# A pre-LN FNet and GEGLU block on one core: an eighth pass of the sequence DFT as seven block products, its operand sums moved to GpSimd

## The chip, the cores and the metric

The kernel runs on one core of one Trainium2 chip. The metric is the device time of one execution in microseconds (us), the median of several runs. In the profile PE is TensorE (its matmuls), PEld its weight loads, DVE is VectorE, ACT is ScalarE, POOL is GpSimd and SP is SyncE, which issues the DMAs here.

## The reference

Sequence S = 2048, model width D = 448, hidden width 1792, all float32.

```python
def _A_ref(x, dft_seq_re, dft_seq_im, dft_hid_re, dft_hid_im):
    a = jnp.einsum("bsd,ed->bse", x, dft_hid_re)
    b = jnp.einsum("bsd,ed->bse", x, dft_hid_im)
    y = jnp.einsum("ts,bse->bte", dft_seq_re, a) - jnp.einsum("ts,bse->bte", dft_seq_im, b)
    return y
def _B_ref(x, w_gate, w_up, w_down):
    g = jnp.einsum("bsd,df->bsf", x, w_gate)
    u = jnp.einsum("bsd,df->bsf", x, w_up)
    return jnp.einsum("bsf,fd->bsd", _gelu(g) * u, w_down)
h = x + _A_ref(_layernorm(x), ...)
h2 = h + _B_ref(_layernorm(h), ...)
```

## The kernel before

**Precision.** Every float32 operand of a matmul is held as two float16 numbers, a high part (`hi_part`, an ACT copy, line 108) and a low part, the operand less its high part (`lo_part`, DVE, lines 112 and 114). A product is three matmuls: high by high, high by low, low by high.

**Stages.** The kernel turns the order of the two DFTs: it multiplies the sequence DFT matrix by the normed x first (results `zs`), transposes them by DMA (`z_turn`), multiplies by the hidden DFT matrix (`hid_mm`, line 731) and adds x. That gives h, whose norm feeds the gate, up and down projections, the rest of the program. The change is in the first part, the 64 steps (`N_STEPS`) of the loop over `n`.

**Steps.** Steps 0 to 15 do the first two of eight pairs of output blocks together. The other six pairs p = 2 to 7 have two passes each (`part`), twelve passes of four steps. A plain pass has 24 matmuls of 448 columns a step (`seq_mm`, line 645). From step `FAST` = 36 on a pass is done as seven block products of Strassen's kind: the four blocks of a 2x2 split are combined in advance, so that seven products of blocks do for eight, and a step has 42 matmuls of 224 columns (`fast_mm`, line 521). Before, five passes are plain and seven are of that kind.

**What a pass of seven products needs.** On the weight side, for each step, three sums on DVE (`fast_sums`, lines 471 to 473) and the splitting of raw and summed blocks (`fast_raw`, `fast_split`). On the x side four sums T1 to T4 for each of eight pairs j of x's blocks, made once: `t_load` fetches two blocks of x again by DMA, `t_norm` norms them on ACT (line 393), `t_sums` makes four sums of 224 columns on DVE (lines 579 to 582), `t_hi` (ACT) and `t_lo` (DVE) split them into the tiles `t`. This happens once for each j, at steps 17 to 37. Step n of such a pass uses the pairs j = 2(n mod 4) and j + 1, in its two halves. At the end of a pass `fast_out` adds the seven sums up (line 550) and `fast_halves` splits them into `zs`.

**What sets the order.** Nothing schedules the program: each engine does its instructions in the order in which the code is written. At step n the code writes first the splitting of the weights for step n + 3 (`seq_hi`, `seq_lo`; n + 2 in the fast passes), then the entries of the table `early` for n, then the matmuls, with the entries of the table `after` for (n, half) behind each half of them. Most work beside the matmuls is placed by these two tables: `at(early, n, ...)` and `at(after, (n, half), ...)`. So an instruction of ACT, DVE or POOL that waits holds up all that the code writes behind it for that engine.

**The hidden matmul and its seed.** `hid_mm(p, g)` runs twice for each p, g = 0 and 1, and both use one PSUM bank. `hid_seed` (ACT, line 712) first puts x into that bank; `hid_out` (ACT, lines 720 to 722) reads the sum and its moments, and only then can ACT seed the bank for g = 1. For p = 0, 1 and 2 the two lie at steps (19, 20), (24, 25) and (29, 30). After the second, `ffn_rstd` makes the scale of the norm: a root on ACT, a reciprocal on DVE (line 203), five small instructions on POOL (lines 204 to 208). For p up to 3 the normed rows are split and transposed in the same steps (`ffn_norm_act`, `ffn_sums`, `ffn_split`, `ffn_transpose`).

**Other work in these steps.** Eight of the fourteen chunks of gate and up weights are summed, split and stored to DRAM (`Weights`: `sums`, `split`, `store`; tiles `gu_s`, `gu_w`), at the steps in the table `DFT_F`. `gw_first` fetches two of them back near the end.

Of the kernel before, what the change touches and what calls it, by code (L numbers as in the profile page):

```python
# [13 lines left out]
P = 128  # L14
# [7 lines left out]
NB = 4  # L22
# [10 lines left out]
def kernel(  # L33
# [76 lines left out]
    def lo_part(dst, src, hi, scale=1.0):  # L110
        if isinstance(scale, float) and scale == 1.0:
            V.tensor_sub(dst, src, hi)  # L112
        else:
            V.scalar_tensor_tensor(dst, src, scale, hi, op0=ALU.mult, op1=ALU.subtract)  # L114
# [113 lines left out]
    def ffn_bias(q, j):  # L228
        mv, r = moments[q, j]
        if q < 2:  # L230
            G.tensor_mul(mv[:, :, 1], mv[:, :, 0], r)
            return
        sign = -1.0 if (q, j) == (NB - 1, 1) else 1.0
        V.scalar_tensor_tensor(mv[:, :, 1], mv[:, :, 0], sign, r, op0=ALU.mult, op1=ALU.mult)

    def ffn_norm_act(q, j, h):

        tag = f"h{q}_{j}"
        mv, r = moments.pop((q, j))
# [152 lines left out]
    def x_affine(dst, src, i):  # L392
        A.activation(dst, src, AF.Identity, scale=affine[:, i, 0:1], bias=affine[:, i, 1:2])
# [55 lines left out]

    FAST = N_STEPS - 28
    A_RAW = ("A12", "A11", "A22")
    FORMS = ("S3", "S1", "S2", "S4")
    T_OPS = ("T1", "T3", "T4", "T2")
    PRODUCTS = ("A11", "B11"), ("A12", "B21"), ("S2", "T2"), ("S3", "T3"), ("S1", "T1"), ("S4", "B22"), ("A22", "T4")
    fast_w, fast_s, fast_t, fast_acc, fast_e = {}, {}, {}, {}, {}

    def fast_views(n):
        raw = wr[n].rearrange("p (i b t) -> p i b t", i=2, b=4)  # L460
# [69 lines left out]
    def fast_halves(n):  # L530
        p, part, qq = step_of(n)
        hi, lo = [zs[p][:, :, l, part * D : (part + 1) * D] for l in range(2)]
        src = fast_e[n][:, 0 : 2 * D].rearrange("p (g d) -> p g d", g=2)
        hi_part(hi, src)
        lo_part(lo, src, hi)

    def fast_out(n, k):

# [25 lines left out]

    tx = {}

    def t_load(j):
        tx[j] = [dft.tile([P, 1, D], F32, tag="xt", bufs=3, name=f"tx{j}_{k}")[:, 0, :] for k in range(2)]
        for k in range(2):
            i = 2 * j + 1 - k  # L570
            nc.sync.dma_start(tx[j][k], x[i * P : (i + 1) * P, :])

    def t_norm(j):
        for k in range(2):
            x_affine(tx[j][k], tx[j][k], 2 * j + 1 - k)

    def t_sums(j):
        (o1, o2), (e1, e2) = [(t[:, 0:HD], t[:, HD:D]) for t in tx[j]]
        V.tensor_sub(o1, o2, o1)
        V.tensor_sub(o2, e2, o2)  # L580
        V.tensor_sub(e2, o1, e2)
        V.scalar_tensor_tensor(e1, e2, -1.0, e1, op0=ALU.mult, op1=ALU.subtract)

    def t_tile(j):

        if j < 4:
            k = j // 2
            if j % 2 == 0:
                fast_t[f"w{k}"] = ring.tile([P, 8 * D], F16, tag=f"w{2 - k}", bufs=1, name=f"t{j}_{j + 1}")
            return fast_t[f"w{k}"][:, j % 2 * 4 * D : (j % 2 + 1) * 4 * D]  # L590
        if j in (4, 5):
            if j == 4:
                fast_t["45"] = dft.tile([P, 8 * D], F16, tag="zs_b", name="t45")
            return fast_t["45"][:, (j - 4) * 4 * D : (j - 3) * 4 * D]
        if j == 6:
            return ring.tile([P, 4 * D], F16, tag="xh4", bufs=1, name="t6")
        return prep.tile([P, 4 * D], F16, tag="raw", bufs=2, name="t7")

    def t_views(j, l):
        return [fast_t[j][:, (2 * l + k) * D : (2 * l + k + 1) * D] for k in range(2)]  # L600
# [153 lines left out]
    def at(where, n, *what):  # L754
        where.setdefault(n, []).extend(what)
# [17 lines left out]

    for f, n in ((0, N_STEPS - 7), (1, N_STEPS - 3)):
        at(after, (n, 1), lambda f=f: gw_first(f))

    turns = [(16, 0), (20, 1), (25, 1), (32, 0), (40, 0), (48, 0), (57, 0)]
    for p, (n, half) in enumerate(turns):
        b, j = divmod(p, 2)
        m = (19, 24, 29, 36, 44, 52, 60)[p]  # L780
        last = ((20, 0), (25, 0), (30, 0), (38, 0), (48, 0), (56, 0), (61, 1))[p]
        m1 = last[0] + 1
        at(early, m - 4, lambda b=b, j=j: h_tile(b, j))
        at(early, m - 2, lambda p=p: hid_seed(p, 0))
        for g in range(2):

            place = last if g else (m, 0)
            at(after, place, lambda p=p, g=g: hid_mm(p, g), lambda p=p, g=g: hid_out(p, g))
            if g == 0:
                at(after, (m, 0), lambda p=p: hid_seed(p, 1))  # L790
        at(after, (n, half), lambda p=p: z_turn(p))
        at(early, m1 + p // 3 if p < 5 else N_STEPS - 7 + p, lambda b=b, j=j: ffn_rstd(b, j))
        at(after, (m1, 0), lambda b=b, j=j: h_store(b, j))
        if b < 2:

            m += 4 if p == 3 else 0
            at(early, m + 2, lambda b=b, j=j: ffn_bias(b, j), lambda b=b, j=j: ffn_norm_act(b, j, hp[b, j]))
            at(early, m + 3, lambda b=b, j=j: ffn_sums(b, j))
            at(early, m + 4, lambda b=b, j=j: ffn_split(b, j))
            for k in range(4):  # L800
                at(after, (m + 5 + k // 2, k % 2), lambda b=b, j=j, k=k: ffn_transpose(b, j, (k,)))
    at(after, (N_STEPS - 6, 0), lambda: gu.update({JIT_F[0]: Weights(JIT_F[0], JIT_F[0] % 3)}))
    at(early, N_STEPS - 2, lambda: h_tile(NB - 1, 1))
    at(early, N_STEPS - 1, gelu_table)
    at(after, (N_STEPS - 2, 0), lambda: down_load(0), lambda: down_load(1))
    for j, n in ((0, 17), (1, 20), (4, 23), (5, 26), (6, 29), (2, 31), (3, 34), (7, 37)):
        at(after, (n - 2, 1), lambda j=j: t_load(j))
        at(early, n, lambda j=j: t_norm(j), lambda j=j: t_sums(j))
        at(after, (n, 0), lambda j=j: t_hi(j))
        at(after, (n, 1), lambda j=j: t_lo(j))  # L810


    fast_at = [FAST + n for n in (-4, -2, -1)] + list(range(FAST + 1, N_STEPS - 2))
# [35 lines left out]
    for n in range(N_STEPS):  # L849
# [88 lines left out]
        for half in range(2):  # L938
            for key, unit, block, c, terms in one[half * len(one) // 2 : (half + 1) * len(one) // 2]:
                seq_mm(key, ws[unit], block, c, terms)  # L940
                if c == NT - 1 and 2 in terms and (n < NT or block in (5, 7)):
                    z_out(*key)
            for what in after.get((n, half), ()):
                what()
    z_turn(NP - 1)
    down_sums(0)
    gu[JIT_F[1]] = Weights(JIT_F[1], JIT_F[1] % 3)

# [330 lines left out]
    for q, t0, step, when in ((2, 5, 3, AT_A), (3, 14, 6, AT_B)):  # L1279
# [22 lines left out]
    right.close()  # L1302
    ps_ff = {
        tag: ctx.enter_context(tc.tile_pool(name=f"ps_{tag}", bufs=1, space=bass.MemoryType.PSUM, reuse_waits="tile"))
        for tag in ("Y", "X", "a0", "a1", "a2", "a3", "Z")
    }
    ps_ff["tr"] = ps_tr

# [272 lines left out]
```

## Time and profile before

| what | value |
|---|---|
| median of 3 runs | 701.28 us (701.15 to 701.37) |
| the profiled execution | 701.11 us |
| its span, first to last instruction | 699.3 us |
| granted clock of TensorE | 1.000 |
| busy PE, DVE, ACT, POOL | 99%, 80%, 57%, 15% of the span |
| plain sequence passes, line 645 | 864 matmuls, 164.7 us busy |
| passes of seven products, line 521 | 1176 matmuls, 144.7 us busy (80.4 and 64.3) |
| hidden matmul, line 731 | 336 matmuls, 66.2 us busy |

The profile is of one execution. A row of the timeline has the start in us from the span's start, the duration, the engine, the source line, the operation, what it writes and reads, the shape, the count of equal instructions merged into the row, and in brackets the idle time of the engine before it with what ended it. The durations of matmuls overlap each other, so the pace of PE is read from the starts of rows. The durations of DVE and ACT overlap by some 0.08 us for the same reason.

### The profile page before, as it was taken

How to read it: one execution, taken by the hardware profiler on the slowest of the kernel's cores; microseconds unless marked ns; L12 is line 12 of the kernel's file. 1: busy time of each engine (PE TensorE's matmuls, PEld its weight loads, DVE VectorE, ACT ScalarE, POOL GpSimd, SP SyncE). 2: the span in 40 equal slices, each digit the busy share in tenths (PEclk: the TensorE clock that was granted, in tenths of full speed). 3: DMA queues.
4: the chain of work that ended last, by engine and by line, in shares of the span. 5: the costliest groups of instructions: out<-in, count | busy, mean ns of one | idle time of the engine just before them, and what ended most of it. 6: DMA issues, size and time to landing. Idle time of an engine off the chain costs nothing.

```text
span 699.3 us, 13800 instructions
## 1 busy us (share of the span) xinstructions
PE 694.1 (99%) x5236; PEld 506.9 (72%) x5236; DVE 556.3 (80%) x1150; ACT 402.1 (57%) x789; POOL 106.7 (15%) x127
## 2 busy tenths in 40 slices
PE   8999999999999999999999999999999999999998
PEld 5555555555579888997644444469999999999997
DVE  7998766865899999985548798786777867899786
ACT  5877566675585556554427666655555453655631
POOL 0000000000001001000303333521120211232224
PEclk9999999999999999999999999999999999999999
DMA  8788888999876477374766878797879995877612
GB/s 276 244 238 284 242 290 215 328 279 294 221 216 166 122 196 199 124 210 174 148 226 230 284 241 251 191 334 234 216 227 331 243 302 174 321 277 273 231 42 80
DMA packets 116179, 160.40 MB, mean 229 GB/s; under 512 B 61968, under 2 KB 80528, under 8 KB 116112
## 3 DMA queue, kind: packets, MB, share of 16 engines
q1 hardware_dynamic: 116112, 159.51, 74.5%
q8 instruction: 41, 0.67, 0.4%
q14 instruction: 26, 0.21, 0.1%
HBM read 111.25 MB, written 34.34 MB: 208 GB/s over the span
## 4 chain that ended last, share of the span: by engine, by line
PE 94%; DVE 2%; ACT 2%; issue 1%; DMA 0%; POOL 0%; DVEq 0%; ACTq 0%; POOLq 0%
PE acc L645 20%; PE acc_f L521 16%; PE acc_d L1243 15%; PE pY L1039 15%; PE pZ L1039 10%; PE pX L1039 10%; PE y L731 9%; DVE gu_w L114 0%; ACT ws L108 0%; DMA x<-in_x_dram 0%; DVE ws L114 0%; DVE xs L112 0%; ACT y L722 0%; ACT hx L720 0%; ACT dn_w L108 0%
## 5 line engine op out<-in xcount | busy, mean ns | idle before, releaser
L1039 PEld LDWEIGHTS <-gw 128*128 128x128 f16 x1404 | 137.1, 98 | 47.0
L645 PE MATMUL acc<-xs,ws 128*128 128x448 f16 x864 | 164.7, 352 | 0.5 <-DVE xs L149 0.5
L645 PEld LDWEIGHTS <-ws 128*128 128x128 f16 x864 | 84.5, 98 | 79.5 <-ACT ws L108 0.6
L521 PEld LDWEIGHTS <-ws 128*128 128x128 f16 x1176 | 112.7, 98 | 1.6
L1243 PE MATMUL acc_d<-wd,dn_w 128*128 128x224 f16 x1008 | 110.6, 259 | 0.0
L1243 PEld LDWEIGHTS <-dn_w 128*128 128x128 f16 x1008 | 96.9, 98 | 1.9
L1133 POOL TENSOR_TENSOR hs<-hs,c 128x256 f32<-128x256 f32 (+1 forms) x42 | 59.8, 1423 | 247.9 <-ACT c L1131 182.0
L1039 PE MATMUL pY<-hops,gw 128*128 128x256 f16 (+1 forms) x612 | 94.2, 296 | 0.0
L114 DVE SCALAR_TENSOR_TENSOR ws<-wr,ws 128x1024 f16<-128x1024 f32 (+2 forms) x66 | 70.9, 1076 | 14.2 <-ACT ws L108 13.7
L521 PE MATMUL acc_f<-t,ws 128*128 128x224 f16 x672 | 80.4, 259 | 0.0
L731 PE MATMUL y<-wh,z 128*128 128x448 f16 x336 | 66.2, 352 | 0.1
L1039 PE MATMUL pZ<-hops,gw 128*128 128x256 f16 (+1 forms) x396 | 64.4, 296 | 0.0
L1039 PE MATMUL pX<-hops,gw 128*128 128x256 f16 (+1 forms) x396 | 64.4, 296 | 0.0
L521 PE MATMUL acc_f<-xs,ws 128*128 128x224 f16 x504 | 64.3, 259 | 0.0
L108 ACT ACTIVATE ws<-wr 128x1024 f16<-128x1024 f32 (+2 forms) x66 | 61.1, 927 | 4.5 <-DMA wr<-in_w_seq_dram 3.2
L1084 ACT ACTIVATE pY<-pX 128x256 f32<-128x256 f32 (+1 forms) x42 | 18.4, 439 | 66.9 <-PE pX L1039 66.5
L731 PEld LDWEIGHTS <-z 128*128 128x128 f16 x336 | 32.8, 98 | 29.6 <-issue 0.3
L1095 ACT ACTIVATE u<-pY 128x256 f32<-128x256 f32 (+1 forms) x42 | 19.1, 454 | 53.6 <-PE pY L1039 53.5
L1049 DVE SCALAR_TENSOR_TENSOR c<-pZ,u 128x256 f32<-128x256 f32 (+1 forms) x42 | 21.4, 510 | 35.4 <-PE pZ L1039 19.3
L108 ACT ACTIVATE ws<-sums 128x512 f16<-128x512 f32 x56 | 34.4, 626 | 24.3 <-DVE sums L471 19.4
L1039 PEld LDWEIGHTS <-gu_w 128*128 128x128 f16 x234 | 22.9, 98 | 27.6
L112 DVE TENSOR_TENSOR dn_w<-dn_s,dn_w 128x640 f16<-128x640 f32 x48 | 41.6, 868 | 1.5 <-ACT dn_w L108 1.4
(145 smaller groups left out, 931.9 us busy)
## 6 DMA issues: line engine op xcount, KB each, us to landing
gw<-w_dram SPq DMA_DIRECT2D x36, 896.0 KB, 6.2
wr<-in_w_seq_dram SPq DMA_DIRECT2D x100, 256.0 KB, 4.5
hid_dram<-hs SPq DMA_DIRECT2D x27, 512.0 KB, 5.7
hid<-hid_dram SPq DMA_DIRECT2D x54, 256.0 KB, 5.4
w_dram<-gu_w SPq DMA_DIRECT2D x14, 896.0 KB, 5.5
gu_raw<-in_w_gu_dram SPq DMA_DIRECT2D x28, 384.0 KB, 5.6
wr<-in_w_seq_dram SPq DMA_DIRECT2D x14, 512.0 KB, 5.2
x<-in_x_dram SPq DMA_DIRECT2D x16, 224.0 KB, 3.8
```

The costliest lines, as they stand in the source:

```text
L108: A.activation(dst, src, AF.Copy, scale=scale)
L112: V.tensor_sub(dst, src, hi)
L114: V.scalar_tensor_tensor(dst, src, scale, hi, op0=ALU.mult, op1=ALU.subtract)
L521: PE.matmul(fast_sum(n, k), fast_a(n, i, lw, a), fast_b(j, lx, b), start=j == 0 and m == 0 and k in (0, 1, 3, 5), stop=j == NT // 2 - 1 an ...
L645: PE.matmul(acc[key][:, :D], w[:, lw, block * P : (block + 1) * P], xs[c][:, lx, :], start=c == 0 and m == 0, stop=c == NT - 1 and m == 2,)
L731: PE.matmul(y[:, :D], z[p][:, lz, k, g * P : (g + 1) * P], wh[:, lw, k, :], start=p == NP - 1 and k == 0 and m == 0, stop=k == 6 and m == ...
L1039: PE.matmul(ps, w[:, wl, wa + ws, :], ops[:, m + ms, :], start=first and n == 0, stop=last and n == len(terms) - 1, skip_group_check=True,)
L1049: V.scalar_tensor_tensor(dst, ps, SC, other, op0=ALU.mult, op1=ALU.add)
L1084: A.activation(self.Y, self.X, AF.Copy)
L1095: A.activation(self.u2, self.Y, AF.Copy, scale=SC)
L1133: G.tensor_mul(c22, c22, self.cols(self.c12))
L1243: PE.matmul(ps, w[:, la, a, :], wd[n][:, lb, b, :], start=n == 0 and m == 0 and opens, stop=n == NC - 1 and m == 2, skip_group_check=True,)
```

## The change

- `FAST` is 32 for 36: the pass of steps 32 to 35 becomes one of seven products, the eighth. Four plain passes are left.
- x is no longer loaded and normed again. `t_sums` now forms normed x as the sum of its two float16 halves in `xs`, and then the four sums, all on GpSimd: two additions of 448 columns, four operations of 224 columns and a change of sign of 224 columns for each j. The result lies in one tile, `xh2` (one buffer; three buffers of one block each before). `t_hi` stays on ACT and `t_lo` on DVE.
- The eight j come at steps 14, 16, 18, 20, 22, 24, 28 and 31 in another order, `t_hi` half a step and `t_lo` a step behind `t_sums`.
- The low half of a pass's result (`lo_part` of `fast_halves`) is put behind the next step's weight sums on DVE.
- Weight chunks 1 and 0 move to other steps; chunk 0 stays in its buffer, so that its first fetch is left out.
- The norm and split of h for p = 1 to 3 move by some steps; the last block of x for h is loaded after the loop, and the second chunk of late weights before its end; the PSUM banks of the later stage are opened in another order.

```diff
-    FAST = N_STEPS - 28
+    FAST = N_STEPS - 32
...
-        lo_part(lo, src, hi)
+        last_lo.append(lambda: lo_part(lo, src, hi))
...
-    def t_load(j):
-        tx[j] = [dft.tile([P, 1, D], F32, tag="xt", bufs=3, name=f"tx{j}_{k}")[:, 0, :] for k in range(2)]
+    def t_sums(j):
+        t = ring.tile([P, 2, D], F32, tag="xh2", bufs=1, name=f"tx{j}")
+        tx[j] = [t[:, k] for k in range(2)]
         for k in range(2):
             i = 2 * j + 1 - k
-            nc.sync.dma_start(tx[j][k], x[i * P : (i + 1) * P, :])
-
-    def t_norm(j):
-        for k in range(2):
-            x_affine(tx[j][k], tx[j][k], 2 * j + 1 - k)
-
-    def t_sums(j):
+            G.tensor_add(tx[j][k], xs[i][:, 0], xs[i][:, 1])
         (o1, o2), (e1, e2) = [(t[:, 0:HD], t[:, HD:D]) for t in tx[j]]
-        V.tensor_sub(o1, o2, o1)
-        V.tensor_sub(o2, e2, o2)
-        V.tensor_sub(e2, o1, e2)
-        V.scalar_tensor_tensor(e1, e2, -1.0, e1, op0=ALU.mult, op1=ALU.subtract)
+        G.tensor_sub(o1, o2, o1)
+        G.tensor_sub(o2, e2, o2)
+        G.tensor_sub(e2, o1, e2)
+        G.tensor_add(e1, e1, e2)
+        G.tensor_scalar(e1, e1, -1.0, None, op0=ALU.mult)
...
-    DFT_F = ((13, 14, 0), ..., (3, 24, 1), (0, 28, 0), (1, 32, 0))
+    DFT_F = ((13, 14, 0), ..., (3, 24, 1), (1, 27, 0), (0, 30, 0))
...
-    for f, n in ((0, N_STEPS - 7), (1, N_STEPS - 3)):
-        at(after, (n, 1), lambda f=f: gw_first(f))
+    at(after, (N_STEPS - 3, 1), lambda: gw_first(1))
...
-    for j, n in ((0, 17), (1, 20), (4, 23), (5, 26), (6, 29), (2, 31), (3, 34), (7, 37)):
-        at(after, (n - 2, 1), lambda j=j: t_load(j))
-        at(early, n, lambda j=j: t_norm(j), lambda j=j: t_sums(j))
-        at(after, (n, 0), lambda j=j: t_hi(j))
-        at(after, (n, 1), lambda j=j: t_lo(j))
+    for j, n in ((6, 14), (7, 16), (0, 18), (1, 20), (4, 22), (5, 24), (2, 28), (3, 31)):
+        at(early, n, lambda j=j: t_sums(j))
+        at(after, (n, 1), lambda j=j: t_hi(j))
+        at(after, (n + 1, 0), lambda j=j: t_lo(j))
...
             fast_sums(unit)
+            while last_lo:
+                last_lo.pop()()
```

How the order of instructions changes is shown on ACT and GpSimd. In the names a first number is the step, chunk or pair that a tile belongs to (`ws21`: weights of step 21; `t0_1`: the tile of pairs 0 and 1), the last number only counts tiles.

ACT before, steps 17 to 19: from the seed of p = 0 to the reading of its first hidden matmul.

```order
L712 ACTIVATE y_0_0_1075<-hx0_0_969 128x448
L393 ACTIVATE tx0_0_1014<-tx0_0_1014,affine_166 128x448
L393 ACTIVATE tx0_1_1015<-tx0_1_1015,affine_166 128x448
L108 ACTIVATE t0_1_1099<-tx0_0_1014 128x448
L108 ACTIVATE t0_1_1099<-tx0_1_1015 128x448
L108 ACTIVATE ws21_1119<-wr21_1020 128x1024
L108 ACTIVATE gu_w11_1070<-gu_s11_1030 128x512 x2
L108 ACTIVATE ws22_1162<-wr22_1064 128x1024
L108 ACTIVATE gu_w9_1165<-gu_raw9_991 128x512
L108 ACTIVATE gu_w9_1165<-gu_raw9_991 128x256
L108 ACTIVATE zs2_1182<-acc2_00_1018 128x448
L720 ACTIVATE hx0_0_969,mv_h0_0_1210<-y_0_0_1075 128x448
```

The same place after the change.

```order
L708 ACTIVATE y_0_0_1095<-hx0_0_980 128x448
L108 ACTIVATE ws21_1130<-wr21_1029 128x1024
L108 ACTIVATE gu_w11_1090<-gu_s11_1039 128x512 x2
L108 ACTIVATE t0_1_1174<-tx0_1142 128x448 x2
L108 ACTIVATE ws22_1180<-wr22_1084 128x1024
L108 ACTIVATE gu_w9_1183<-gu_raw9_1002 128x512
L108 ACTIVATE gu_w9_1183<-gu_raw9_1002 128x256
L108 ACTIVATE zs2_1200<-acc2_00_1027 128x448
L716 ACTIVATE hx0_0_980,mv_h0_0_1228<-y_0_0_1095 128x448
```

The two norms are gone, and the split of `t0_1` now stands behind the weights of step 21 and ahead of those of step 22 and of the first reading of `y_0_0`. Its input `tx0` comes from GpSimd. GpSimd, which had nothing to do between the start of the program and the first `r_h`, now has this at steps 16 and 18.

```order
L572 TENSOR_TENSOR tx7_1044<-xs15_893 128x448
L572 TENSOR_TENSOR tx7_1044<-xs14_844 128x448
L574 TENSOR_TENSOR tx7_1044<-tx7_1044 128x224
L575 TENSOR_TENSOR tx7_1044<-tx7_1044 128x224
L576 TENSOR_TENSOR tx7_1044<-tx7_1044 128x224
L577 TENSOR_TENSOR tx7_1044<-tx7_1044 128x224
L578 TENSOR_SCALAR tx7_1044<-tx7_1044 128x224
L572 TENSOR_TENSOR tx0_1142<-xs1_223 128x448
```

Pair 0 takes up the buffer of pair 7, so its first row comes after DVE has read pair 7 for the last time (`t_lo`).

More of the change, by code (lines that the diff above doesn't have):

```diff
@@ L456 @@
     PRODUCTS = ("A11", "B11"), ("A12", "B21"), ("S2", "T2"), ("S3", "T3"), ("S1", "T1"), ("S4", "B22"), ("A22", "T4")
-    fast_w, fast_s, fast_t, fast_acc, fast_e = {}, {}, {}, {}, {}
+    fast_w, fast_s, fast_t, fast_acc, fast_e, last_lo = {}, {}, {}, {}, {}, []
     def fast_views(n):
@@ L596, in t_tile @@
             return ring.tile([P, 4 * D], F16, tag="xh4", bufs=1, name="t6")
-        return prep.tile([P, 4 * D], F16, tag="raw", bufs=2, name="t7")
+        return ring.tile([P, 4 * D], F16, tag="xh3", bufs=1, name="t7")
     def t_views(j, l):
@@ L748 @@
     gu, gw = {}, {}
-    DFT_F = ((13, 14, 0), (11, 16, 1), (9, 18, 0), (7, 20, 1), (5, 22, 0), (3, 24, 1), (0, 28, 0), (1, 32, 0))
+    DFT_F = ((13, 14, 0), (11, 16, 1), (9, 18, 0), (7, 20, 1), (5, 22, 0), (3, 24, 1), (1, 27, 0), (0, 30, 0))
     JIT_F = range(2, 13, 2)
@@ L768 @@
         at(early, n, lambda f=f: gu[f].sums())
+        if f == 0:
+            at(early, n + 2, lambda: gu[0].split(True))
+            at(early, n + 3, lambda: gu[0].split(False), lambda: gw.update({0: gu[0].w}))
+            at(after, (n + 5, 0), lambda: gu[0].store())
+            continue
         at(early, n + 1, lambda f=f: gu[f].split(True))
@@ L794 @@
         if b < 2:
[L796 to L799, printed above, removed]
+            n0, n1, n2 = ((21, 22, 23), (26, 27, 29), (36, 37, 38), (44, 45, 46))[p]
+            at(early, n0, lambda b=b, j=j: ffn_bias(b, j), lambda b=b, j=j: ffn_norm_act(b, j, hp[b, j]))
+            at(early, n1, lambda b=b, j=j: ffn_sums(b, j))
+            at(early, n2, lambda b=b, j=j: ffn_split(b, j))
             for k in range(4):
-                at(after, (m + 5 + k // 2, k % 2), lambda b=b, j=j, k=k: ffn_transpose(b, j, (k,)))
+                at(after, (n2 + 1 + k // 2, k % 2), lambda b=b, j=j, k=k: ffn_transpose(b, j, (k,)))
+    at(after, (N_STEPS - 5, 0), lambda: gu.update({JIT_F[1]: Weights(JIT_F[1], JIT_F[1] % 3)}))
     at(after, (N_STEPS - 6, 0), lambda: gu.update({JIT_F[0]: Weights(JIT_F[0], JIT_F[0] % 3)}))
-    at(early, N_STEPS - 2, lambda: h_tile(NB - 1, 1))
     at(early, N_STEPS - 1, gelu_table)
     at(after, (N_STEPS - 2, 0), lambda: down_load(0), lambda: down_load(1))
-    for j, n in ((0, 17), (1, 20), (4, 23), (5, 26), (6, 29), (2, 31), (3, 34), (7, 37)):
-        at(after, (n - 2, 1), lambda j=j: t_load(j))
-        at(early, n, lambda j=j: t_norm(j), lambda j=j: t_sums(j))
-        at(after, (n, 0), lambda j=j: t_hi(j))
-        at(after, (n, 1), lambda j=j: t_lo(j))
+    for j, n in ((6, 14), (7, 16), (0, 18), (1, 20), (4, 22), (5, 24), (2, 28), (3, 31)):
+        at(early, n, lambda j=j: t_sums(j))
+        at(after, (n, 1), lambda j=j: t_hi(j))
+        at(after, (n + 1, 0), lambda j=j: t_lo(j))
     fast_at = [FAST + n for n in (-4, -2, -1)] + list(range(FAST + 1, N_STEPS - 2))
@@ L944 @@
                 what()
+    last_lo.pop()()
     z_turn(NP - 1)
     down_sums(0)
-    gu[JIT_F[1]] = Weights(JIT_F[1], JIT_F[1] % 3)
+    h_tile(NB - 1, 1)
     seq.close()
@@ L1304 @@
         tag: ctx.enter_context(tc.tile_pool(name=f"ps_{tag}", bufs=1, space=bass.MemoryType.PSUM, reuse_waits="tile"))
-        for tag in ("Y", "X", "a0", "a1", "a2", "a3", "Z")
+        for tag in ("a0", "a1", "a2", "a3", "Z", "Y", "X")
     }
```

## The prediction

> **What bounds the kernel now.** I read the shares of busy time first, then PE's timeline, what PE waits for, and the chain of waits in the steps that change.
>
> ```profile
> PE 694.1 (99%) x5236; PEld 506.9 (72%) x5236; DVE 556.3 (80%) x1150; ACT 402.1 (57%) x789; POOL 106.7 (15%) x127
> ```
>
> PE is the bound: no other engine is near its 99%. PE's timeline, around the hidden matmuls of p = 0 and 1 (L731):
>
> ```profile
> 102.99 4.13 PE L731 MATMUL y<-wh,z 128*128 128x448 f16 x21
> 106.96 18.32 PE L645 MATMUL acc<-xs,ws 128*128 128x448 f16 x96
> 125.12 4.14 PE L731 MATMUL y<-wh,z 128*128 128x448 f16 x21
> 129.09 4.70 PE L645 MATMUL acc<-xs,ws 128*128 128x448 f16 x24
> 133.89 4.13 PE L731 MATMUL y<-wh,z 128*128 128x448 f16 x21
> 164.53 4.14 PE L731 MATMUL y<-wh,z 128*128 128x448 f16 x21
> 199.48 0.74 PE L521 MATMUL acc_f<-xs,ws 128*128 128x224 f16 x6
> 201.49 0.74 PE L521 MATMUL acc_f<-xs,ws 128*128 128x224 f16 x6
> ```
>
> The pace is read from starts. A plain pass, 96 matmuls of L645, takes 125.12 - 106.96 = 18.16 us, a step 4.54; a hidden matmul takes 129.09 - 125.12 = 3.97. The last two rows start two halves of a fast step: 2.01 a half, 16.08 for a pass.
>
> One place has no slack. The hidden matmul at 133.89 should start at 129.09 + 4.54 = 133.63. The chain of waits leaves PE there:
>
> ```profile
> 133.29 0.56 ACT y L712
> 133.89 4.13 PE y L731 x21
> ```
>
> PE waits for the seed, which ACT puts into the bank at 133.29: 0.26 us late already. In the plain passes PE waits for nothing else of size:
>
> ```profile
> L645 PE MATMUL acc<-xs,ws 128*128 128x448 f16 x864 | 164.7, 352 | 0.5 <-DVE xs L149 0.5
> ```
>
> **What is sure.** One plain pass becomes a fast one: 18.16 - 16.08 = 2.08 us less on PE, with no idle time of PE at the passage between the two kinds. The sixteen loads of x, the norms on ACT and chunk 0's fetch leave engines and queues for which PE does not wait: nothing. The later move of `lo_part`, the PSUM order and the tail loads: nothing, PE's work there being queued ahead. If all else holds, the profiled execution's 701.11 (span 699.3, 1.8 around it; 0.17 under the median) becomes 699.0.
>
> **The price of `t_sums` on GpSimd.** No GpSimd sum of this form stands in the trace; the nearest are late weight sums, first alone, then beside DVE:
>
> ```profile
> 336.70 1.14 POOL L225 TENSOR_TENSOR wd_s<-wd 128x448 f32<-128x448 f32 x1
> 337.79 0.66 POOL L226 TENSOR_TENSOR wd_s<-wd 128x224 f32<-128x224 f32 x1
> 440.10 1.58 POOL L223 TENSOR_TENSOR wd_s<-wd 128x448 f32<-128x448 f32 x1
> 441.64 1.84 POOL L225 TENSOR_TENSOR wd_s<-wd 128x448 f32<-128x448 f32 x1
> 443.45 0.71 POOL L226 TENSOR_TENSOR wd_s<-wd 128x224 f32<-128x224 f32 x1
> 440.61 1.88 DVE L112 TENSOR_TENSOR xs<-tt,xs 128x768 f16<-128x768 f32 x1
> 442.42 1.22 DVE L112 TENSOR_TENSOR xs<-xn_h,xs 128x128 f16<-128x128 f32 x1
> L204 POOL TENSOR_SCALAR r_h<-mv_h 128x2 f32<-128x2 f32 x7 | 1.9, 278 | 264.1 <-ACT y L722 264.0
> ```
>
> Alone a tile costs 2 x 1.10 + 4 x 0.62 + the change of sign. That lies between 0.20 (the last row, two columns) and 0.66; I take 0.4, since it reads one input. Sum 5.1. Beside DVE the two engines take turns: POOL's end 441.68, DVE's 442.49, POOL's 443.48, DVE's 443.64. DVE's 128 columns, on the face of it a short instruction, took 1.22 of which most is POOL's turn. From 442.49 to 443.48 the turn of POOL's 448 columns is 0.99; I take 1.0 for 448 columns in turns and, by half, 0.5 for 224. If seven DVE instructions stand between, as step 18's, which run from 89.97 to 94.17 (rows below, 4.2 us), a tile costs 4.4 + 4.2 less an overlap of 0.3 = 8.3 us. So 5.1 to 8.3, nearer 8.3 where DVE is dense.
>
> The Trainium skill ("SBUF — State Buffer", "Who interferes with whom") says that of a DVE operation with two SBUF inputs and a GpSimd operation reading SBUF the one that starts first holds the shared port pair for its whole instruction. The rows agree in the kind, the turns; but by its words GpSimd would hold its full 5.1 us, an estimate of 5.1 + 4.2 = 9.3 a tile, and some 1 us later per tile.
>
> **The loop.** `xh2` has one buffer, so one turn is: GpSimd sums, ACT `t_hi`, ACT and then DVE halves of the next weights (in order, so ahead), DVE `t_lo`, next sums. At the steps (19, 20), (24, 25) and (29, 30) ACT's `hid_out` and seed stand behind a `t_hi` that waits for GpSimd. Rows for the durations:
>
> ```profile
> 75.39 4.60 DVE L114 SCALAR_TENSOR_TENSOR zs<-acc,zs 128x448 f16<-128x448 f32 x8 [3.45 <-ACT zs L108]
> 80.31 1.22 DVE L114 SCALAR_TENSOR_TENSOR ws<-wr,ws 128x1024 f16<-128x1024 f32 x1 [0.32 <-ACT ws L108]
> 83.84 0.42 DVE L330 TENSOR_TENSOR gu_s<-gu_raw 128x256 f32<-128x256 f32 x1
> 84.51 1.22 DVE L114 SCALAR_TENSOR_TENSOR ws<-wr,ws 128x1024 f16<-128x1024 f32 x1
> 86.58 0.39 DVE L579 TENSOR_TENSOR tx<-tx 128x224 f32<-128x224 f32 x1
> 89.97 1.23 DVE L114 SCALAR_TENSOR_TENSOR ws<-wr,ws 128x1024 f16<-128x1024 f32 x1 [0.32 <-DMA gu_raw<-in_w_gu_dram]
> 94.17 1.22 DVE L114 SCALAR_TENSOR_TENSOR ws<-wr,ws 128x1024 f16<-128x1024 f32 x1
> 109.35 1.16 DVE L112 TENSOR_TENSOR t<-tx,t 128x448 f16<-128x448 f32 x2 [0.97 <-ACT t L108]
> 90.88 1.04 ACT L108 ACTIVATE ws<-wr 128x1024 f16<-128x1024 f32 x1
> 91.83 0.92 ACT L108 ACTIVATE gu_w<-gu_raw 128x512 f16<-128x512 f32 x2
> 94.68 0.54 ACT L108 ACTIVATE zs<-acc 128x448 f16<-128x448 f32 x1 [1.93 <-PE acc L645]
> 98.65 0.54 ACT L720 ACTIVATE hx<-y 128x448 f32<-128x448 f32 x1 [3.43 <-PE y L731]
> 100.31 0.55 ACT L712 ACTIVATE y<-hx 128x448 f32<-128x448 f32 x1
> 108.75 1.03 ACT L108 ACTIVATE t<-tx 128x448 f16<-128x448 f32 x2
> 78.59:100.72 22.13, 22.13 (x118) 11.45 (x117) 17.15 (x30) 13.67 (x26) 0.00 (x0) 1.00 0.94 290
> ```
>
> *First seed.* `t_lo` of pair 6 stands behind four of the `zs` rows: 75.39 + 2.3 + 1.1 = 78.7. Sums of pair 7: two additions before DVE's row at 80.31 end at 80.95; the other five (2.4) beside DVE's 80.31 to 83.84 (3.5) end at 86.85. `t_hi` 1.0, ws 0.95, DVE's halves 84.51 to 86.58 = 2.07, `t_lo` 1.1: 92.0. Sums of pair 0, 8.3: 100.3. `t_hi` 1.0, ws and gu_w 1.9, zs 0.5: 103.7. `hid_out` and seed, 98.65 to 100.86: 105.9. PE wants it at 102.99: **2.9 us late**.
>
> *Second.* Two more turns of 1.0 + 0.95 + 2.07 + 1.1 + 8.3, with five small GpSimd operations of 0.28 (L204's row), end pair 4's sums at 128.4. ACT then has `t_hi` 1.0, two steps' weights 3.8, the high parts of h (1600 columns at ws's rate, 1.8) and two zs 1.0: 136.0. The seed 2.2 gives 138.2, against 133.89 + 2.9: **1.4 late**.
>
> *Third.* Behind `t_hi` of pair 4 come ACT's 6.6, DVE's low parts of h (some 2), zs and `t_lo`: 136.7. Pair 5's sums: 145.0. `t_hi` and one step's weights 2.8, `hid_out` 2.0, weights 1.9: the root at 151.7, DVE's reciprocal 153.0, GpSimd's five 154.4. DVE's work from there to step 32's weight sums is some 9.1 us by its rows, and pair 2's sums between them hold it up by 4.4: 166.5 to 167. ACT's remaining 5.2 give 172, the seed 174.3. PE wants it at 164.53 + 2.9 + 1.4 = 168.8: **5.6 late**.
>
> That is 9.9 with DVE dense. The last row above, steps 16 to 19 by windows (PE, PEld, DVE, ACT, POOL), has DVE busy 17.15 of 22.13, 78%. With GpSimd alone the same sums keep all three seeds in time, 1.4 to spare at the third. I take 78% of the way from -1.4 to 9.9: **7.4 us**.
>
> **The last pair.** Pair 3 (step 31) stands on GpSimd behind the scale of p = 2, whose root needs the second hidden matmul, done at 164.53 + 3.97 = 168.5. `hid_out` 1.7, two weights 1.9, root and reciprocal 1.3, GpSimd's small ones 1.1: 174.5. Sums alone 5.1, `t_hi` 1.0, a gu_w half 0.9, DVE's low half and `t_lo` 1.8 to 2.6: 183.3 to 184.1. Step 33, the first user, wants the tile a step of 4.02, a half of 2.01 and six matmuls (0.57) after the pass's start, which is 168.5 + 1.5 plain steps = 175.3: 181.9. **1.8 late**, and all in relation to PE's own hidden matmul, so earlier stalls do not hide it. Below: 0, if `hid_out` and the weights overlap better; above: 5, with turns.
>
> **DVE in the fast passes.** One more fast pass means more DVE work on the weights. The rows are the groups by form in 40 to 340 us, and one of the timeline:
>
> ```profile
> L471 DVE TENSOR_TENSOR sums<-wr 128x512 f32<-128x512 f32 x28 | 19.1, 684 | 0.0
> L472 DVE TENSOR_TENSOR sums<-sums,wr 128x256 f32<-128x256 f32 x28 | 11.9, 425 | 1.0
> L473 DVE TENSOR_TENSOR sums<-wr,sums 128x256 f32<-128x256 f32 x28 | 11.9, 425 | 1.0
> L114 DVE SCALAR_TENSOR_TENSOR ws<-wr,ws 128x768 f16<-128x768 f32 x28 | 26.6, 951 | 0.1
> 249.56 1.22 DVE L114 SCALAR_TENSOR_TENSOR ws<-sums,ws 128x1024 f16<-128x1024 f32 x1
> ```
>
> A fast unit costs 0.68 + 2 x 0.43 + 0.95 + 1.22 = 3.7 us, a plain one 1.22, so four of them 9.9 more. The weights of the last row, step 47's, are ready at 250.78, just ahead of PE, so any net increase by then would be paid. But DVE has lost `t_sums`' 8 x 4 x 0.39 = 12.5 us (row at 86.58), and ACT lost the norms. I put it at 0; it can't be below, since PE has no gap there to give back, and 2 above if GpSimd's turns delay the units early.
>
> **Sum.** 701.11 - 2.1 + 7.4 + 1.8 = **708.2 us**.
>
> **Rivals.** *Faster, 0.30.* GpSimd's operations fall into the 22% of DVE's time that is idle and into its PSUM-reading instructions, and DVE runs far enough ahead: the seeds hold, step 33 is late by 0.7 at most. For: ACT has the norms less, PE waits 3 steps behind the weights. Against: the 0.26 above, at a seed that now stands behind two `t_hi`. It gives 698.9 to 699.8. *No change, 0.15.* The seeds hold, but the last pair's 1.8 or so eats the 2.1: 700.0 to 702.4, likeliest 700.8. *Slower, 0.55*, the forecast, from the point where the stalls exceed 3.5: 703 to 712.5. Its upper end is 699.0 + 9.9 + 3.6, turns everywhere and at the last pair in part. That the change does not do what it says I leave at nothing: the order of instructions shows it.
>
> A measurement of this kernel can tell about 0.2%, 1.4 us, from no change. The range must take in both signs: 698.9 to 712.5.
>
> **What would show it.** Right: `t_sums` rows with 448 columns of 1.5 us and more and a tile of 7 to 8 us between 78 and 160; PE idle at the second hidden matmuls of p = 0, 1, 2, put down to ACT's seed, growing from one to the third; a wait in step 33 for `t`. Wrong: tiles of 5 to 6 us, hidden matmuls that start 4.54 after the step ahead of them, and PE busy at 99% with a span of 697.2; or a wait at step 47's weights, which would put the bound on DVE.

## The result and the profile after

The changed kernel takes 708.94 us (median of 4 runs, 707.77 to 709.24) against 701.33 us for the kernel before (701.15 to 701.89) on the same chip: ratio 1.0104, 95% interval 1.0087 to 1.0122. The profiled execution took 708.71 us with a span of 706.9 us. The forecast of 708.2 us was right, and so was its sign.

The page of the profile after: span, then busy time by engine.

```profile
span 706.9 us, 13957 instructions
PE 695.0 (98%) x5308; PEld 514.2 (73%) x5308; DVE 571.7 (81%) x1137; ACT 393.7 (56%) x781; POOL 163.4 (23%) x183
```

PE is busy about as long as before (694.1 us), though it has 2.1 us less to do, because a part of its work runs at a lower clock; and it now waits. What PE waits for, in us in total, times, longest:

```profile
PE y L727 <- ACT y L708: 5.6, 2, 4.2
PE acc_f L521 <- DVE t L112: 1.4, 1, 1.4
```

L708 is `hid_seed` (its line moves with every edit: L711 to L725 in the kernels below), L112 the low part (`t_lo`). PE's timeline shows where. The first two pairs of rows are the first and second seed, then the third, then step 33:

```profile
98.42 4.70 PE L641 MATMUL acc<-xs,ws 128*128 128x448 f16 x24
104.53 4.13 PE L727 MATMUL y<-wh,z 128*128 128x448 f16 x21 [1.41 <-ACT y L708]
130.63 4.70 PE L641 MATMUL acc<-xs,ws 128*128 128x448 f16 x24
135.23 4.13 PE L727 MATMUL y<-wh,z 128*128 128x448 f16 x21
161.33 4.70 PE L641 MATMUL acc<-xs,ws 128*128 128x448 f16 x24
170.25 6.53 PE L727 MATMUL y<-wh,z 128*128 128x448 f16 x21 [4.22 <-ACT y L708]
176.62 6.97 PE L641 MATMUL acc<-xs,ws 128*128 128x448 f16 x36
191.72 0.93 PE L521 MATMUL acc_f<-t,ws 128*128 128x224 f16 x8 [1.42 <-DVE t L112]
```

A step is 4.54 us, so the hidden matmuls start 1.57, 0.06 and 4.38 us after the step ahead of them has ended. The third also takes 176.62 - 170.25 = 6.37 us where the others take 3.97: 2.40 more. The windows around it (length, busy PE, PEld, DVE, ACT, POOL, then the granted clock, DMA share, GB/s) say why:

```profile
161.00:166.00 5.00, 5.00 (x27) 2.49 (x26) 4.90 (x9) 3.65 (x8) 0.00 (x0) 1.00 0.59 209
166.00:170.00 4.00, 0.03 (x1) 0.00 (x0) 3.66 (x9) 3.90 (x11) 0.00 (x0) 0.79 0.67 252
170.00:173.00 3.00, 2.75 (x8) 1.17 (x8) 2.93 (x6) 2.23 (x4) 0.00 (x0) 0.50 1.01 212
173.00:177.00 4.00, 4.00 (x18) 1.78 (x16) 3.93 (x8) 0.12 (x1) 0.00 (x0) 0.73 0.67 181
177.00:183.00 6.00, 6.00 (x33) 3.13 (x32) 3.42 (x6) 3.94 (x10) 1.25 (x6) 1.00 0.59 170
```

The granted clock falls to a half while PE is still idle, and from 177 us on it is at 1.00 again. Taken as time at 1.00 or at 0.50, the rows with 0.79, 0.50 and 0.73 make 6.8 us at a half. For the last 4.9 us of them PE works, at half its pace, which is an estimate of 2.4 us lost.

The account: -2.08 (the pass) + 1.57 + 4.38 + 2.40 + 1.42, less the 0.26 - 0.06 by which the second seed is now better, is 7.5. The spans differ by 7.6. The first matmul of the next stage, before and after:

```profile
337.98 0.19 PE L1082 MATMUL pY<-hops,gw 128*128 128x64 f16 x1
```

```profile
345.58 0.19 PE L1084 MATMUL pY<-hops,gu_w 128*128 128x64 f16 x1
```

It is also 7.6 us later, so nothing was won or lost behind the sequence DFT.

GpSimd's sums, one tile beside a busy DVE (pair 0, first and last row) and the one that ran nearly alone (pair 3):

```profile
91.61 3.32 POOL L572 TENSOR_TENSOR tx<-xs 128x448 f32<-128x448 f16 x2 [4.97 <-ACT gu_w L108]
...
98.75 0.82 POOL L578 TENSOR_SCALAR tx<-tx 128x224 f32<-128x224 f32 x1
182.71 2.02 POOL L572 TENSOR_TENSOR tx<-xs 128x448 f32<-128x448 f16 x2
...
187.63 0.77 POOL L578 TENSOR_SCALAR tx<-tx 128x224 f32<-128x224 f32 x1
```

8.0 us for the first, 5.7 for the second; the other six take 7.0 to 7.9.

### The profile page after: what moved, and what is told of

Read it like the earlier page. It is cut to its first block, busy times and chain, and to the rows that moved or that the text cites. A ratio compares the mean times of both kernels' runs of the same rounds, so it can differ in the third digit from the quotient of the medians.

```text
span 706.9 us, 13957 instructions
## 1 busy us (share of the span) xinstructions
PE 695.0 (98%) x5308; PEld 514.2 (73%) x5308; DVE 571.7 (81%) x1137; ACT 393.7 (56%) x781; POOL 163.4 (23%) x183
## 4 chain that ended last, share of the span: by engine, by line
PE 82%; DVE 4%; DMA 4%; POOL 3%; SPq 2%; ACT 2%; issue 2%; DVEq 0%; ACTq 0%; POOLq 0%
PE acc_f L521 17%; PE acc_d L1245 15%; PE pY L1041 15%; PE acc L641 10%; PE pX L1041 9%; PE pZ L1041 9%; PE y L727 7%; DMA wr<-in_w_seq_dram 2%; DVE gu_w L114 1%; POOL tx L572 1%; DMA gu_raw<-in_w_gu_dram 1%; DVE zs L114 1%; DMA w_dram<-gu_w 1%; SPq L666 1%; DVE t L112 1%
## 5 line engine op out<-in xcount | busy, mean ns | idle before, releaser
L1041 PEld LDWEIGHTS <-gw 128*128 128x128 f16 x1365 | 133.1, 98 | 43.0 <-DMA gw<-w_dram 0.2
L641 PE MATMUL acc<-xs,ws 128*128 128x448 f16 x768 | 146.6, 353 | 0.3 <-DVE xs L149 0.3
L521 PEld LDWEIGHTS <-ws 128*128 128x128 f16 x1344 | 128.8, 98 | 3.2 <-issue 1.6
L641 PEld LDWEIGHTS <-ws 128*128 128x128 f16 x768 | 75.0, 98 | 70.6 <-ACT ws L108 0.4
L521 PE MATMUL acc_f<-t,ws 128*128 128x224 f16 x768 | 92.1, 259 | 1.4 <-DVE t L112 1.4
L1041 PE MATMUL pY<-hops,gw 128*128 128x256 f16 (+1 forms) x595 | 90.2, 294 | 0.0
L114 DVE SCALAR_TENSOR_TENSOR ws<-wr,ws 128x768 f16<-128x768 f32 (+2 forms) x66 | 71.0, 1077 | 19.0 <-ACT ws L108 18.6
L521 PE MATMUL acc_f<-xs,ws 128*128 128x224 f16 x576 | 73.5, 259 | 0.0
L108 ACT ACTIVATE ws<-wr 128x768 f16<-128x768 f32 (+2 forms) x66 | 60.3, 914 | 11.7 <-DMA wr<-in_w_seq_dram 11.1
L108 ACT ACTIVATE ws<-sums 128x512 f16<-128x512 f32 x64 | 38.6, 623 | 25.2 <-DVE sums L471 20.8
L1041 PEld LDWEIGHTS <-gu_w 128*128 128x128 f16 x273 | 26.6, 98 | 31.9
L112 DVE TENSOR_TENSOR dn_w<-dn_s,dn_w 128x640 f16<-128x640 f32 x48 | 42.3, 880 | 1.5 <-ACT dn_w L108 1.4
```

The source lines that it names most:

```text
L108: A.activation(dst, src, AF.Copy, scale=scale)
L521: PE.matmul(fast_sum(n, k), fast_a(n, i, lw, a), fast_b(j, lx, b), start=j == 0 and m == 0 and k in (0, 1, 3, 5), stop=j == NT // 2 - 1 an ...
L641: PE.matmul(acc[key][:, :D], w[:, lw, block * P : (block + 1) * P], xs[c][:, lx, :], start=c == 0 and m == 0, stop=c == NT - 1 and m == 2,)
L1041: PE.matmul(ps, w[:, wl, wa + ws, :], ops[:, m + ms, :], start=first and n == 0, stop=last and n == len(terms) - 1, skip_group_check=True,)
```

## The experiments

The theory at the start: GpSimd takes turns with DVE, the loop through the one buffer `xh2` gets slow, and `t_hi` holds ACT up ahead of the seeds. The rivals: the order of the other work that was moved is to blame, or the share of SBUF costs by itself, whoever waits for the sums. All ratios are to the kernel before in the same job.

### The sums on DVE

```diff
-            G.tensor_add(tx[j][k], xs[i][:, 0], xs[i][:, 1])
+            V.tensor_add(tx[j][k], xs[i][:, 0], xs[i][:, 1])
...
-        G.tensor_scalar(e1, e1, -1.0, None, op0=ALU.mult)
+        V.tensor_scalar(e1, e1, -1.0, None, op0=ALU.mult)
```

> The seven operations of t_sums go to DVE at the same places in the order (a tile then costs 2 x 0.62 + 4 x 0.39 + 0.19 = 3.0 us instead of 7 to 8). If GpSimd's turns with DVE and the loop through xh2 make the seeds late: no stall at the first and second seed, 0 to 3 us at the third (DVE still has 3.0 us more there), the stall of step 33 under 0.5; 701 us (699 to 704). If the order of the other work (norms and splits of h, weight sums from step 28 on) makes them late and GpSimd is innocent: 707 to 710, as after the change.

714.12 us, ratio 1.0186 (1.0169 to 1.0203): both expectations missed, and worse than with GpSimd. What PE waits for:

```profile
PE y L727 <- ACT y L708: 11.4, 3, 6.0
```

Three seeds are late, by 2.86, 2.51 and 6.00 us. DVE in 78.59 to 100.72 us is busy 20.20 us of 22.13 (17.15 before the change). DVE's own time at these steps is what is short; GpSimd's turns are one way to take it, more work on DVE another, here the dearer one.

### The kernel before with GpSimd sums that nobody reads

The sums of the change, word for word, into a tile of their own, at the change's steps:

```diff
+    for j, n in ((6, 14), (7, 16), (0, 18), (1, 20), (4, 22), (5, 24), (2, 28), (3, 31)):
+        at(early, n, lambda j=j: g_sums(j))
```

> The kernel before, with the eight GpSimd sums of the change added at the same steps into a tile that nobody reads. If it is the path through t_hi that costs: DVE's instructions grow by 3 to 4 us for each sum but PE hardly waits; 701 to 702 us. If sharing SBUF with DVE costs by itself: the same loss as after the change at the seeds, 704 us or more.

709.22 us, 1.0113 (1.0098 to 1.0128). Sharing by itself costs as much as the change did. The first row is DVE's window of steps 16 to 19, to be held against 17.15 busy us and 30 instructions before; the second what PE waits for:

```profile
78.59:100.72 22.13, 22.13 (x119) 11.45 (x118) 21.33 (x31) 13.56 (x26) 13.24 (x14) 1.00 1.05 294
```

```profile
PE y L744 <- ACT y L725: 6.0, 2, 5.0
```

DVE is busy 4.2 us more for one instruction more. The longer stall is at another seed than after the change (the second of p = 1, 5.03 us): there ACT splits a pair whose sums DVE made late.

```profile
133.03 0.58 ACT L108 ACTIVATE t<-tx 128x448 f16<-128x448 f32 x1 [3.02 <-DVE tx L580]
```

From the low parts of a weight chunk to the first sum of that pair DVE took 8.7 us before (117.97 to 126.65); beside GpSimd's sums it takes 13.6 (118.54 to 132.12) and does not stand idle. GpSimd's own queue is not to blame: its part of the scale of p = 0 ends 11.4 us after the second hidden matmul of p = 0 starts (103.52 to 114.94), as before (102.99 to 114.40). So the one buffer and the reader are not needed for a loss of this size; the slowed DVE is enough.

### Half of the sums' work

The two additions of 448 columns are left out; the sums are made from the high half of x alone, so the low half is missing from them.

```diff
-            G.tensor_add(tx[j][k], xs[i][:, 0], xs[i][:, 1])
...
-        G.tensor_sub(o1, o2, o1)
+        h = [xs[2 * j + 1 - k][:, 0] for k in range(2)]
+        (a1, a2), (b1, b2) = [(t[:, 0:HD], t[:, HD:D]) for t in h]
+        G.tensor_sub(o1, a2, a1)
```

> The two additions of 448 columns are left out: the sums are made from the high half of x alone, so the low half is missing from T1 to T4. A tile costs GpSimd some 4.2 us in turns, 3.3 alone. If the loop through GpSimd is the cause: first and second seed in time, third 0 to 2 us late, no wait in step 33; 699.0 to 701 us. If the order of the other work is the cause: 706 us or more.

699.07 us, 0.9970 (0.9958 to 0.9982), as the theory said; PE waits at no seed and not in step 33. The order of the other work is thus not to blame by itself, and the pass is worth the 2.1 us that the prediction gave it.

### Seven passes, with the sums on GpSimd

```diff
-    FAST = N_STEPS - 32
+    FAST = N_STEPS - 28
```

> The pass of steps 32 to 35 is plain again, all else as after the change. If GpSimd's sums are the cause: the first seed stays 1.4 us late, the third 0 to 2 us late (the weight sums of step 28 are gone from DVE), step 33 waits for nothing; 702 to 704 us. If the added fast pass is the cause: no stall at all, 701.1 us.

706.63 us, 1.0082 (1.0063 to 1.0102): more than expected. The first seed is 1.41 us late, as with eight passes, the third 1.99, and the clock fell behind it (that hidden matmul took 5.82 us instead of 4.13). Without the added pass the sums alone cost 5.4 us: they are the larger part of the loss. But the pass is no gain here either: with it the loss is 7.6 us. The third seed is 4.22 us late instead of 1.99, where the weights of the pass's first steps are what is added ahead of it, and step 33 waits.

### x loaded and normed again

Eight passes, but x fetched by DMA and normed by ACT as before the change; the four sums on DVE, or with the change of sign on GpSimd.

```diff
+        at(after, (n - 2, 1), lambda j=j: t_load(j))
-        at(early, n, lambda j=j: t_sums(j))
+        at(early, n, lambda j=j: t_norm(j), lambda j=j: t_sums(j))
```

> Eight passes, but x is loaded and normed again as before the change (two buffers in turn), and the four sums are on DVE as before. GpSimd has none of it; DVE has 1.56 us for each pair where sums_on_dve had 3.0. If the work on DVE and GpSimd together decides: seeds in time or late by under 1 us in all, 699 to 700.5 us. If any sum on DVE at these steps is too much: 703 us or more.

> As x_again_dve, with the four sums and the change of sign on GpSimd (the two additions of 448 columns are replaced by the load and ACT's norm). Same result as the whole of x in the sums, same GpSimd work as high_half_sums: if the time that GpSimd holds DVE up decides, 699.0 to 699.8 us, as there. If the saving there came from reading float16 or from leaving the load out: 701 us or more.

708.11 us (1.0090, 1.0078 to 1.0103) and 710.25 us (1.0137, 1.0122 to 1.0153): the theory missed both, and both times lie in the range of its rivals. GpSimd does five instructions per tile here as in the version with half the work, and the kernel is 11 us slower. Reading float16 is not what saved time there: the sums of pair 2 take 4.0 us here and 4.3 there. The chain of waits of the GpSimd version, into its third seed (6.95 us late):

```profile
153.96 6.34 DMA wr<-in_w_seq_dram
...
163.49 0.66 ACT tx L393
...
164.22 0.92 POOL tx L583
...
167.49 0.78 POOL tx L587
...
173.15 0.56 ACT y L717
```

The chain begins with a load: ACT waits 4.78 us for the weights of step 32, which it splits at step 28 (3.49 after the change). Its norm of pair 2 stands behind these weights, GpSimd's sums wait for the norm, and ACT's split and then the seed wait for the sums. In the DVE version (third seed 5.73 us late) the sums stand behind the same weights in DVE's queue. From `xs` the sums could start when GpSimd was free, long before ACT came to that step (at 150.86 after the change, 164.22 here). So where in the queues the sums may start counts too, not only their amount; that the load of x also fills SP's queue was not separated from it.

### Two buffers for the sums

Every other tile goes to two blocks of the buffer of x, free by then.

```diff
+        if j in (6, 0, 4, 2):
+            t = ring.tile([P, 2, D], F32, tag="xh2", bufs=1, name=f"tx{j}")
+            tx[j] = [t[:, k] for k in range(2)]
+        else:
+            tx[j] = [dft.tile([P, 1, D], F32, tag="xt", bufs=3, name=f"tx{j}_{k}")[:, 0, :] for k in range(2)]
```

> As after the change, but the sums alternate between xh2 and two blocks of the three-block buffer of x, free by then, so that the sums of one pair no longer wait for the low part of the pair before. If the loop through the one buffer makes the seeds late: the first seed in time, the third under 1.5 us late; 701 to 704 us. If it is the time that DVE and GpSimd hold the shared input together, and not the loop: the sums start earlier but DVE stays as late; the seeds change by less than 1 us; 707 to 709.5 us.

706.81 us, 1.0076 (1.0063 to 1.0088). What PE waits for:

```profile
PE y L730 <- ACT y L711: 3.8, 1, 3.8
PE acc_f L521 <- DVE t L112: 1.4, 1, 1.4
```

Each expectation was met in part. The first seed is in time: its 1.4 us were the loop's. DVE is busy 21.99 of the 22.13 us from 78.59 to 100.72 here, so a full DVE alone does not make that seed late; it matters what stands ahead of the seed. The third, 3.81 us late, and step 33 have another cause.

### The third seed

Its rows after the change, on ACT and in what SP's queue waited for from 100 to 170 us (after, then before):

```profile
159.06 0.84 ACT L108 ACTIVATE ws<-wr 128x768 f16<-128x768 f32 x1 [3.49 <-DMA wr<-in_w_seq_dram]
162.06 0.63 ACT L108 ACTIVATE ws<-sums 128x512 f16<-128x512 f32 x1 [2.16 <-DVE sums L471]
169.66 0.55 ACT L708 ACTIVATE y<-hx 128x448 f32<-128x448 f32 x1
```

```profile
SPq L323 <- DVE gu_w L114: 7.4, 1, 7.4
SPq L323 <- DVE xs L112: 5.7, 1, 5.7
SPq L432 <- DVE ws L114: 4.8, 1, 4.8
```

```profile
SPq L670 <- PE y L731: 8.5, 1, 8.5
SPq L305 <- DVE tx L582: 2.4, 1, 2.4
```

Before, SP's longest wait was for PE. After, it waits for DVE again and again, and its loads and stores come late. Two kernels move what stands ahead of that seed. The first puts the weights of the first fast steps behind it. The second also has the two buffers and the sums of pair 3 at step 29, ahead of GpSimd's part of the scale of p = 2.

```diff
-    fast_at = [FAST + n for n in (-4, -2, -1)] + list(range(FAST + 1, N_STEPS - 2))
+    fast_at = [FAST + n for n in (-2, -1, 0)] + list(range(FAST + 1, N_STEPS - 2))
```

> As after the change, but the weights of the first three fast steps are summed and split at steps 30, 31 and 32 for 28, 30 and 31, so that they stand behind hid_out and seed of p = 2 on ACT and DVE. If the third seed is late because it stands behind these weights (whose DMA and DVE sums come late): first seed 1.4 us late as before, third under 1 us, step 33 as before or 1 us worse; 702 to 704 us. If it is late because of the pair split ahead of it (t_hi of pair 2) or the split of h: third seed still 3 us or more late; 707 us or more.

> Eight passes with all three stalls aimed at: two buffers for the sums, the first fast weights two steps later, the sums of pair 3 at step 29, ahead of the scale of p = 2 on GpSimd. If each stall is what its wait names: PE waits under 0.5 us in all at the seeds and in step 33; 699.0 to 699.8 us, faster than both kernels. If the turns of DVE and GpSimd make something else late instead (the weights of the fast steps, which then wait for DVE): 701 us or more.

710.92 us (1.0131, 1.0114 to 1.0148) and 705.32 us (1.0057, 1.0044 to 1.0069). The first expectation fails for both: the third seed is still 3.54 and 3.50 us late, with the weights gone from ahead of it. Step 33's wait is gone in the second, and 4.28 us in the first. What ACT waits for in the second, from 140 to 185 us:

```profile
ACT t L108 <- DMA w_dram<-gu_w: 6.0, 1, 6.0
```

The split of pair 2 takes over a weight chunk's buffer (`t_tile`: tag `w1`), and the store of that chunk stands in SP's late queue. The next kernel puts this split behind the seed too; the last one then takes the move of the weights back.

```diff
     for j, n in ((6, 14), (7, 16), (0, 18), (1, 20), (4, 22), (5, 24), (2, 28), (3, 29)):
         at(early, n, lambda j=j: t_sums(j))
-        n += j == 3
+        n += j in (2, 3)
         at(after, (n, 1), lambda j=j: t_hi(j))
         at(after, (n + 1, 0), lambda j=j: t_lo(j))
```

> As three_moves, with the split of pair 2 (t_hi and t_lo) a step later, behind hid_out and seed of p = 2. In three_moves ACT waits there 6.0 us for the store of a weight chunk whose buffer the split takes over. If that wait alone makes the third seed late: third seed in time, no fall of the clock, PE waits under 1 us in all; 699.0 to 700.0 us. If the seed has a second cause of about the same date (weights by DMA, the split of h): 0.5 to 3 us late still; 701 to 704 us.

> As split_behind_seed, with the first fast weights back at steps 28, 30 and 31. If the third seed is late for two reasons of about the same date (the split of pair 2 waiting for a store, and step 28's fast weights waiting for their DMA and DVE's sums): third seed still 1.5 to 3 us late, as two_buffers less the 1.3 us of the split; 701 to 704 us. If the wait of the split alone decides: 698.8 us, as there.

The first takes **698.82 us**, 0.9965 (0.9952 to 0.9979): faster than both kernels. All that PE waits for in it is at the start and the end of the program:

```profile
PE pw L102 <- POOL sign_t L93: 1.4, 1, 1.4
PE acc_d L1249 <- ACT v L975: 0.2, 1, 0.2
```

The second takes 702.44 us, 1.0024 (1.0013 to 1.0034), with the third seed 2.53 us late:

```profile
158.96 0.84 ACT L108 ACTIVATE ws<-wr 128x768 f16<-128x768 f32 x1 [3.39 <-DMA wr<-in_w_seq_dram]
```

```profile
166.96 4.13 PE L730 MATMUL y<-wh,z 128*128 128x448 f16 x21 [2.53 <-ACT y L711]
```

So the third seed had two causes of about the same date, both by way of SP: the load of step 32's weights and the store that frees the split's buffer. Taking away either one leaves 2.5 to 3.5 us, both together nothing. In the changed kernel ACT also waits for DVE's sums of these weights (2.16 us above), but they are not needed for the lateness: in the last kernel, and with the two buffers alone, DVE itself waits for that load (0.25 and 2.00 us). Whether this seed also needs the two buffers and the early sums of pair 3 was not tried.

### A stall made on purpose

The kernel before, with one seed written ten times more.

```diff
+                if p == 2:
+                    for _ in range(10):
+                        at(after, (m, 0), lambda p=p: A.activation(ys[p, 1][:, :D], hp[p // 2, p % 2][:, 1, :], AF.Copy, scale=sign_of(p, 1) * D_SC))
```

> The kernel before, with the seed of the second hidden matmul of p = 2 written ten times more by ACT (the same values; 0.48 us each, 4.8 us). It has 2.1 us in hand there, so PE stalls 2.7 us once. If a stall costs only itself: 701.2 + 2.7 = 703.9 us. If the granted clock falls behind a stall of this length as behind the 4.2 us one after the change (2.4 us lost): 705 to 706.3 us.

707.43 us (705.00 to 708.81), 1.0082 (1.0063 to 1.0102). The stall was 3.61 us, not 2.7 (a repeated seed takes ACT some 0.57 us), and the median lies above both forecasts. The hidden matmul behind it:

```profile
168.21 5.82 PE L731 MATMUL y<-wh,z 128*128 128x448 f16 x21 [3.61 <-ACT y L793]
```

5.82 for 4.13: the clock's fall is a cost of the stall, in a kernel without any of the change.

## Why the prediction was right

**The pass, -2.08.** Right: 699.07 and 698.82 us where nothing stalls, for 699.0 forecast.

**The price of `t_sums`, 5.1 alone to 8.3 in turns.** Right: 5.7 and 7.0 to 8.0. The change of sign, put at 0.4, takes 0.77 alone, above its upper bound of 0.66; its lower bound of 0.20 stands for a row that says 0.278. What the prediction quoted of the Trainium skill (SBUF — State Buffer, Who interferes with whom) is borne out in its kind: the kernel before with idle sums, where only the sharing differs, has DVE 4.2 us longer busy in 22. The estimate of 9.3 us a tile that the prediction made from it is above every tile of these runs (at most 8.2, waits for a buffer left out).

**First seed, 2.9 dense.** Measured 1.57, by the mechanism named (the two buffers remove it). The sums of pair 0 ran from 91.61 to 99.57, forecast 92.0 to 100.3.

**Second seed, 1.4.** Measured 0.06. Pair 4's sums ended at 126.15, not 128.4: pair 0's had ended 0.7 us early, and the two tiles behind them took 7.9 and 7.4 us for the 8.3 counted. ACT's work behind them, put at 7.6, took 6.8.

**Third seed, 5.6.** The size came near (4.38), the way there was only half right. The weights of step 32 do hold ACT up, but ACT waits 3.49 us for their load first and then 2.16 for DVE's sums. These end at 162.95 where the prediction had 166.5 to 167, with PE 2.9 us ahead of the forecast there. That SP's queue, held up by DVE, brings this load and the store ahead of `t_hi` late is missing from the prediction. It had counted ACT and DVE along the chain and no DMA.

**The discount and its sum, 7.4.** The three stalls make 6.0 (5.8 with the second seed's earlier 0.26 taken off); the fall of the clock, 2.40, was in no term. The total of 8.2 is near 7.4 because the one makes up for the other: that is luck, the sum is better than its parts. The 1.4 us to spare with GpSimd alone, one end of the discount, had no working shown.

**Step 33, 1.8.** Measured 1.42, and the move of pair 3 ahead of the scale removes it, as its place in GpSimd's queue said. **DVE in the fast passes, 0.** Right: no wait there.

**The rivals.** "Faster" needed GpSimd's work to fall into DVE's idle time. That idle time was there, 22% by the window, 5.0 us; the idle sums alone take 4.2 of it, and the seeds come late all the same.

## What to carry to other kernels

Work put on GpSimd is not free where DVE is dense: add a share of DVE's time to its price, and look first at the queue that waits for DVE, the DMA issues among them. To the price of a PE stall of 2 us and more add the clock's fall, 1.3 to 2.6 us here. Where two engines hand work to and fro in a fixed order, find the few places where PE has no slack, and put every wait that does not belong there behind them; a second buffer and a few entries of the tables turned a loss of 7.6 us into a gain of 2.4. A stall with two causes of one date hides both from single experiments: remove them together.

## What the runs showed of the hardware

**The granted clock falls behind a stall of PE.** A hidden matmul that takes 4.13 us took 5.46 to 6.75 behind every stall of 2.86 us and more ahead of a seeded hidden matmul in these runs. Below, it varies: no fall behind 1.41, 1.86, 2.08, 2.51 and 2.53 us, a fall behind 1.99.

Finer windows of the same traces show why. In all twelve falls the clock stood at 0.50 for 3.41 us or for 6.83, twice that, and for no other time. Where one execution has two falls, they begin 68.27 us apart in the version with the sums on DVE (105.79 and 174.06), and 23.89 with the fast weights later (171.20 and 195.09): 20 and 7 times 3.41. So the clock is set at the ends of windows of 3.41 us that run on whatever PE does. The version with the sums on DVE, cut at these ends (two windows with the stall of 2.51 us, then four with that of 6.00):

```profile
136.51:139.92 3.41, 2.10 (x12) 0.98 (x10) 3.41 (x9) 3.35 (x9) 0.00 (x0) 1.00 0.93 301
139.92:143.34 3.42, 2.22 (x12) 1.17 (x12) 3.35 (x6) 1.12 (x3) 0.00 (x0) 1.00 1.14 264
170.65:174.06 3.41, 1.28 (x7) 0.57 (x6) 2.11 (x6) 2.17 (x5) 0.00 (x0) 1.00 0.01 4
174.06:177.48 3.42, 0.00 (x0) 0.00 (x0) 3.08 (x9) 3.32 (x11) 0.00 (x0) 0.50 0.55 220
177.48:180.89 3.41, 2.97 (x9) 1.19 (x9) 3.34 (x7) 2.41 (x4) 0.00 (x0) 0.50 0.96 202
180.89:184.30 3.41, 3.41 (x20) 1.77 (x19) 3.38 (x6) 0.67 (x3) 0.00 (x0) 1.00 0.71 189
```

The stall of 2.51 us lies across an end of a window, 1.31 us on one side and 1.20 on the other, and nothing follows. The longer one leaves PE busy for 1.28 us of one window and for none of the next, and the clock is halved in the window behind each. All twelve falls follow a window in which PE was idle for 1.99 us or more. At the full clock, no fall follows the windows of these stalls with 1.86 us idle or less, nor one with 1.99: the border lies there. So the same stall can cost nothing, or one or two windows at a half, by where it falls. The executions of one kernel fit this: the twelve of the last kernel of the section on the third seed run from 701.35 us, at a mean clock of 1.000, by 703.54 at 0.998, to 705.49 at 0.995, and one window at a half takes 0.5 x 3.41 / 700 = 0.0024 off the mean.

The Trainium skill (TensorE: Matmul & The Clock Gate, What's actually happening) says that the clock is halved after at least one idle window of about 3.4 us, and that the windows run free of the program. The half, the length of the window and its free run agree; but the window need not be idle throughout, since 1.99 us of it were enough once.
